# Linear attention and a highway layer on one core: stacked head pairs, permuted model dimensions, output summed and turned on TensorE, fixed instruction order

## The chip, the cores and the metric

The kernel runs on one core of a Trainium2 chip. Such a core has five engines with an instruction queue each: TensorE (PE, matrix products, its weight loads listed as PEld), VectorE (DVE), ScalarE (ACT), GpSimd (POOL) and SyncE (SP, which here only issues transfers). An engine works through its own queue in order and waits on semaphores for the others. Data lie in SBUF (128 partitions) and in PSUM (eight banks, written by PE); transfers between memory and SBUF run on 16 DMA engines. The metric is the device time of one execution in microseconds (us); less is better.

## The reference

Inputs are `q`, `k`, `v` of shape (8 batches, 8 heads, 576 tokens, 64) in fp32, two weight matrices of 512x512 and a bias of 512. First comes linear attention, then a highway layer on all 8 x 576 = 4608 tokens of 8 x 64 = 512 model dimensions:

```python
q_s = exp(q - max(q, -1));  q_s = q_s / sum(q_s, -1)      # softmax over the 64 dims
k_s = exp(k - max(k, 2));   k_s = k_s / sum(k_s, 2)       # softmax over the 576 tokens
kv  = einsum('bhsd,bhse->bhde', k_s, v)                   # 64 x 64 for each head
x   = einsum('bhsd,bhde->bhse', q_s, kv)                  # tokens x 512
H   = maximum(x @ w_h, 0)
T   = sigmoid(x @ w_t + b_t)
out = T * H + (1 - T) * x
```

The sums can be left to the end: dividing a row of `kv` by the sum of its `exp(k)` column is the same as normalising `k` first. A column of ones beside `v` gives that sum from the same product.

## The kernel before

A batch of 576 tokens is split into 512 (four tokens to a partition) and a rest of 64. `load_batch` (L77) fetches `k` and `q` as fp32 through SP's queue (q1 in the profile) and `v` through GpSimd's queue (q0), which casts it to fp16 on the way; the weights take the same queue (L215, L216). Three sets of input buffers exist. `prelude` (L97) does the exps on ScalarE and, on VectorE, the sums of the query softmax (`qsm`, L112, and `qst` for the rest), their reciprocals and the scaling (`qs16m`, L120).

Attention then goes pair by pair of heads, four pairs to a batch: PE forms `kv` of each head (L260, and L267 for the rest; 64x65 products, ten a pair), turns the scaled queries (L73) into the PSUM tile `qtt`, VectorE takes the reciprocal `rz` (L279), builds the block-diagonal `abk` of the two heads (L281 to L283) and copies the turned queries out as `qsT` (L285). `flush_rb` (L227) multiplies the two (`pxT`, L239), and ScalarE writes the result to `xT` (L247, L248), model dimensions on partitions, tokens along the free axis.

The highway layer works on blocks of 512 tokens, nine of them (`tcn`), which don't line up with the batches of 576. `moe_dc` (L141) takes one 128-wide part of the output dimensions: `psh` and `pst`, four products each (L148, L153); tanh in place of the sigmoid (`th`, L158, since sigmoid(z) = (1 + tanh(z/2))/2); `dd = max(psh, 0) - x` on VectorE (L161); `uu = dd * th` on GpSimd (L163). One part later `moe_flush_pend` (L167) does `ww = uu + dd` (L172) and `gg = 0.5 * ww + x` (L174) on VectorE. `moe_finish` (L177) turns `gg` back to token rows on PE (L73, `nat`), ScalarE copies the rows out (L191), and SP stores them, in 56 stores.

The order on the engines is that of a scheduler working from dependences and priorities; the code runs block `b-1` of the highway layer beside the attention of batch `b`, one part after each head pair, and `prelude(b+1)` after the first pair.

## Time and profile before

| | |
|---|---|
| time, median of 3 runs | 222.51 us (221.66 to 223.78) |
| span of the profiled execution | 219.1 us |
| median time less that span | 3.4 us |
| PE, DVE, ACT, POOL busy | 137.4, 164.5, 102.0, 79.5 us |
| read from memory, written | 30.41 MB, 9.44 MB |

The profile has the span of one execution, from its first to its last instruction; the time of a run holds a few microseconds around it. Busy times of the engines overlap, so they don't add up to the span; the longest of them is a floor, and what is above it are waits. In the rows of groups an entry reads line, engine, operation, output<-input, partitions x elements, count | busy us, mean ns of one | idle us ahead of them and what ended it. A row such as `PEclk` cuts the span into 40 slices of 5.5 us, one digit each.

### The profile page before, as it was taken

The numbers are of one execution on the slowest core, as the hardware profiler recorded it, in microseconds if no ns is written. First come the engines' busy times: TensorE is split into PE (matmuls) and PEld (weight loads), VectorE is DVE, ScalarE is ACT, GpSimd is POOL, SyncE is SP. The second block draws the span as 40 slices with busy tenths as digits, with TensorE's granted clock in tenths as the row PEclk, the third lists the DMA queues.
The fourth block names the chain that finished last, engine by engine and source line by source line (L and its number), as shares of the span: only waits on it lengthen the run. The fifth ranks groups of instructions, "written<-read, shape, count | busy, mean of one in ns | idle before, by whom it ended". The sixth has DMA issues, their size and how long they took to land.

```text
span 219.1 us, 3271 instructions
## 1 busy us (share of the span) xinstructions
PE 137.4 (63%) x1170; PEld 71.3 (33%) x1170; DVE 164.5 (75%) x357; ACT 102.0 (47%) x151; POOL 79.5 (36%) x84
## 2 busy tenths in 40 slices
...
PEclk9855558556999797699589959985996999999955
DMA  6999999999999999997899209920060033071426
GB/s 185 253 211 268 210 249 252 229 270 223 274 221 186 127 280 223 283 112 160 262 254 162 93 0 73 183 47 0 3 193 3 0 120 74 0 195 50 141 56 135
DMA packets 69696, 34.29 MB, mean 157 GB/s; under 512 B 47664, under 2 KB 65072, under 8 KB 69680
## 3 DMA queue, kind: packets, MB, share of 16 engines
q1 hardware_dynamic: 31120, 28.32, 50.4%
q0 software_dynamic: 38560, 5.77, 37.2%
q8 instruction: 9, 0.15, 0.3%
q14 instruction: 7, 0.06, 0.1%
HBM read 30.41 MB, written 9.44 MB: 182 GB/s over the span
## 4 chain that ended last, share of the span: by engine, by line
DVE 38%; DMA 30%; issue 13%; POOL 9%; PE 4%; ACT 2%; ACTq 1%; POOLq 0%; DVEq 0%
DMA v16m<-in_v_dram 30%; DVE gg L174 9%; POOL uu L163 5%; DVE dd L161 5%; DVE qsm L112 5%; DVE ww L172 5%; DVE qsT L285 4%; POOL v16m L88 3%; DVE qs16t L125 2%; DVE abk L283 2%; DVE qst L113 1%; DVE rz L279 1%; PE qtt L73 1%; DVE abk L282 1%; PE nat L73 1%
## 5 line engine op out<-in xcount | busy, mean ns | idle before, releaser
L163 POOL TENSOR_TENSOR uu<-dd,th 128x512 f16<-128x512 f16 x36 | 43.3, 1205 | 79.1 <-DVE dd L161 66.1
L153 PE MATMUL pst<-xT,w16t 128*128 128x512 f16 x144 | 44.8, 415 | 17.7 <-DVE dd L161 17.2
L148 PE MATMUL psh<-xT,w16h 128*128 128x512 f16 x144 | 42.2, 395 | 5.5 <-ACT th L158 3.5
...
L158 ACT ACTIVATE th<-pst,bt 128x512 f16<-128x512 f32 x36 | 24.9, 691 | 32.5 <-PE pst L153 32.5
L174 DVE SCALAR_TENSOR_TENSOR gg<-ww,xT 128x512 f16<-128x512 f16 x36 | 34.8, 966 | 0.3
L247 ACT CAST xT<-pxT 128x512 f16<-128x512 f32 x32 | 18.7, 583 | 27.7 <-PE qtt L243 27.5
L260 PE MATMUL qtt<-v16m,ek16m 128*64 128x65 f16 x256 | 17.6, 224 | 22.2 <-DMA v16m<-in_v_dram 21.4
L260 PEld LDWEIGHTS <-ek16m 128*64 128x64 f16 x256 | 12.4, 129 | 41.3 <-issue 41.1
L112 DVE TENSOR_REDUCE qsm<-eq16m 128x32 f16<-128x2048 f16 x8 | 18.2, 2277 | 9.8 <-ACT eq16m L105 9.7
L172 DVE TENSOR_TENSOR ww<-uu,dd 128x512 f16<-128x512 f16 x36 | 18.7, 520 | 9.0 <-POOL uu L163 8.7
L153 PEld LDWEIGHTS <-w16t 128*128 128x128 f16 x144 | 13.7, 102 | 35.0 <-issue 23.7
L105 ACT ACTIVATE eq16m<-q32m 128x2048 f16<-128x2048 f32 x8 | 15.3, 1907 | 21.0 <-DMA q32m<-in_q_dram 9.3
L161 DVE SCALAR_TENSOR_TENSOR dd<-psh,xT 128x512 f16<-128x512 f32 x36 | 23.9, 664 | 1.1 <-PE psh L148 1.0
L73 PE MATMUL nat<-ident,gg 128*128 128x128 f16 x144 | 16.3, 245 | 12.8 <-DVE gg L174 12.5
L191 ACT CAST o<-nat 128x1024 f32<-128x1024 f16 x18 | 17.4, 1016 | 12.9 <-PE nat L73 12.9
L73 PE MATMUL qtt<-ident,qs16m 128*64 128x128 f16 x256 | 22.5, 258 | 0.0
L103 ACT ACTIVATE ek16m<-k32m 128x2048 f16<-128x2048 f32 x8 | 15.4, 1920 | 13.2 <-DMA k32m<-in_k_dram 12.6
L279 DVE RECIPROCAL rz<-qtt 128x1 f32<-128x1 f32 x32 | 5.2, 162 | 20.0 <-PE qtt L73 19.8
L239 PE MATMUL pxT<-qsT,abk 128*128 128x512 f16 x32 | 14.9, 465 | 6.5 <-ACT xT L247 3.7
L148 PEld LDWEIGHTS <-w16h 128*128 128x128 f16 x144 | 13.2, 100 | 17.3 <-issue 6.3
L285 DVE TENSOR_SCALAR qsT<-qtt,rz 128x640 f16<-128x640 f16 x32 | 17.6, 550 | 1.0
...
## 6 DMA issues: line engine op xcount, KB each, us to landing
...
q32m<-in_q_dram SPq DMA_DIRECT2D x8, 1024.0 KB, 14.2
out_dram<-o SPq DMA_DIRECT2D x40, 128.0 KB, 2.4
v16m<-in_v_dram POOLq DMA_DIRECT2D x32, 128.0 KB, 10.2
out_dram<-o SPq DMA_DIRECT2D x16, 256.0 KB, 2.7
q32t<-in_q_dram SPq DMA_DIRECT2D x8, 128.0 KB, 11.4
k32t<-in_k_dram SPq DMA_DIRECT2D x8, 128.0 KB, 10.3
...
```

Of the source, the lines that this page charges most:

```text
L73: nc.tensor.matmul(out_ap, in_ap, idn, is_transpose=True, start=True, stop=True, skip_group_check=True,)
L88: nc.gpsimd.dma_start(v16m[:, :, j, 0:D], v_m[b][:, :, j, :])
L112: nc.vector.reduce_sum(qsm, eqm_g, axis=mybir.AxisListType.X)
L148: nc.tensor.matmul(psh, w16h[:, kc, dsl], xT[:, kc, tok], start=(kc == 0), stop=(kc == KC - 1),)
L153: nc.tensor.matmul(pst, w16t[:, kc, dsl], xT[:, kc, tok], start=(kc == 0), stop=(kc == KC - 1),)
L158: nc.scalar.activation(th, pst, AF.Tanh, bias=bt2[:, dc : dc + 1], scale=0.5)
L161: nc.vector.scalar_tensor_tensor(dd, psh, 0.0, xs, op0=ALU.max, op1=ALU.subtract)
L163: nc.gpsimd.tensor_mul(uu, dd, th)
L172: nc.vector.tensor_add(ww, uu, dd)
L174: nc.vector.scalar_tensor_tensor(gg, ww, 0.5, xs, op0=ALU.mult, op1=ALU.add)
L260: nc.tensor.matmul(psk[od, :], ek16m[:, h, j, :], v16m[:, h, j, 0 : D + 1], start=(j == 0), stop=False,)
L285: nc.vector.tensor_scalar_mul(qsT, pqt, rz)
```

## The change

The computation is the same; nearly every step is laid out anew.

*Loads.* Partition `64x + p` of an input tile holds head `2c + x`, tokens `9p` to `9p + 8`, for the four pairs `c`, so that nine tokens of a head (2304 bytes) are one piece and no rest of 64 tokens is treated apart. `v` comes as fp32 through SP's queue like `k` and `q`, and GpSimd casts it (`cast_v`, two halves a batch); the weights likewise (`cast_weight`, eight casts in all). GpSimd does nothing else in the main loop.

*Attention.* The exps work on halves of a batch (two head pairs on 128 partitions). `kv_half` forms products of 64 rows by 128 columns by 129: two heads at once, of which only the diagonal blocks are used. `q_sums` adds the halves of 64 in fp16 and reduces 32; `q_mult` scales in place; `q_trans` turns the queries in full 128x128 blocks. `x_blk` is the product with `abk`. The model dimensions stand in another order than in memory (within four heads, the odd ones behind the even ones), which the weights' loading and the order of the output's columns take back.

*Highway layer.* A block of 512 tokens now belongs to one batch (tokens `9p + n` for n up to 7), eight blocks, and the ninth tokens of all batches form the ninth block (`x9`). `moe_step` does tanh on ScalarE, then `dd` and `u = (th + 1) * dd`, both on VectorE. `out_tile` lets PE add and turn in one: `x` times the identity plus `u` times half the identity, summed in PSUM in fp32; ScalarE copies (two tiles of the last four go to VectorE), and SP stores four tokens to a partition at a time, 12 stores.

*Order.* `manual_schedule` keeps the order in which the code issues: in step s (0 to 3) of block c the four engines get `moe_step(c, s)`, quarter s of the attention of batch c+1, quarter s of the exps of batch c+2, and one output tile of an earlier pair of batches. Loads for batch c+3 are issued at the start of block c.

VectorE, around the sums of the query softmax of one batch, before: the two reductions and the scaling come in one piece, and the four small operations of a head pair stand between `dd`, `ww` and `gg`.

```order
L112 TENSOR_REDUCE qsm<-eq16m 128x32
L113 TENSOR_REDUCE qst<-eq16t 64x8
L116 RECIPROCAL rqm<-qsm 128x32
L117 RECIPROCAL rqt<-qst 64x8
L120 TENSOR_TENSOR qs16m<-eq16m,rqm 128x2048
L125 TENSOR_TENSOR qs16t<-eq16t,rqt 64x512
L126 MEMSET qs16t 64x256
L279 RECIPROCAL rz<-qtt 128x1
L281 MEMSET abk 128x64
L161 SCALAR_TENSOR_TENSOR dd<-psh,xT 128x512
```

VectorE after the change, the first half of block 1, with the number of a buffer behind each name: the sums of batch 2 (`l`, `r`) end just ahead, and the scaling of its queries (`eq_470`) stands two MoE steps later.

```order
L198 CAST r_2_508<-r_2_507 128x72
L268 SCALAR_TENSOR_TENSOR dd_0_531<-ph_0_520,xT_305 128x512
L271 SCALAR_TENSOR_TENSOR u_345<-th_0_529,dd_0_531 128x8x64
L268 SCALAR_TENSOR_TENSOR dd_1_568<-ph_1_557,xT_305 128x512
L271 SCALAR_TENSOR_TENSOR u_345<-th_1_566,dd_1_568 128x8x64
L178 RECIPROCAL rz_589<-psk_534 128x4
L182 TENSOR_TENSOR abk_108<-psk_534,rz_589 64x2x2x64 x2
L206 TENSOR_TENSOR eq_470<-eq_470,r_2_508 128x1280
L206 TENSOR_TENSOR eq_470<-eq_470,r_2_508 128x1024
L268 SCALAR_TENSOR_TENSOR dd_2_609<-ph_2_598,xT_305 128x512
```

So the reduction and the scaling of one batch are apart by two MoE steps, and each `dd` is followed at once by its `u`, where `ww` and `gg` waited for GpSimd.

GpSimd in the main loop before: products of the highway layer between the issues of the `v` transfers.

```order
L163 TENSOR_TENSOR uu<-dd,th 128x512 x2
L88 DMA v16m<-in_v_dram 128x8x64 x2
L163 TENSOR_TENSOR uu<-dd,th 128x512
L88 DMA v16m<-in_v_dram 128x8x64 x2
L91 DMA v16t<-in_v_dram 64x8x64
```

GpSimd after the change, from the first cast on.

```order
L156 CAST v_0_110<-v_0_117 128x9x128 x2
L112 CAST w16t<-w32t 128x8x64 x4
L112 CAST w16h<-w32h 128x8x64 x4
L156 CAST v_1_111<-v_1_135 128x9x128 x2
L156 CAST v_0_110<-v_2_341 128x9x128 x2
```

All that is left is casts, two a batch after the weights.

ScalarE at the end, before: two copies of two token tiles each, after four tanh in a row.

```order
L191 CAST o_2294<-nat_0_2060 128x1024
L191 CAST o_2300<-nat_1_2061 128x1024
L158 ACTIVATE th<-pst,bt_100 128x512 x4
L191 CAST o_2403<-nat_0_2305 128x1024
L191 CAST o_2407<-nat_1_2306 128x1024
```

ScalarE at the end, after the change (`o_3_4` is the buffer for tiles 4 to 7 of batches 6 and 7, `o_0_8` that for the ninth tokens of batches 0 and 1; the last number is the tile's own).

```order
L266 ACTIVATE th_2_1888<-pt_2_1878,bt_107 128x512
L296 COPY o_3_4_1902<-nat_4_1893 128x512
L296 COPY o_3_4_1902<-nat_5_1904 128x512
L266 ACTIVATE th_3_1924<-pt_3_1914,bt_107 128x512
L296 COPY o_3_4_1902<-nat_6_1929 128x512
L296 COPY o_3_4_1902<-nat_7_1939 128x512
L296 COPY o_0_8_1959<-nat_8_1950 128x512
L296 COPY o_2_8_1983<-nat_8_1974 128x512
```

Copies of one tile each, two to a step in the last block, and the tiles of the ninth tokens of all batches at the very end (those of pairs 1 and 3 on VectorE).

The added lines, with the constants, the weights' loading and the views of a block left out; the removed ones are the listing above.

```diff
...
+    def heads_view(t, b):
+        return t[b].rearrange("(c x) (p n) d -> (x p) c (n d)", x=2, n=N9)
...
+    ld = pool("ld", 3)
...
+    og = pool("og", 2)
+    ps_ht = pool("ps_ht", 3, space=PSUM)
+    ps_kv = pool("ps_kv", 1, space=PSUM)
+    ps_q = pool("ps_q", 2, space=PSUM)
+    ps_nat = pool("ps_nat", 1, space=PSUM)
+
+    ctx.enter_context(tc.manual_schedule())
...
+    def load(b, which, halves=1):
+        dst, src, tag = {
+            "k": (k32, k, "k32"), "q": (q32, q, "q32"), "v": (v32, v, "v32"),
+        }[which]
+        t = ld.tile([P, 4, N9, 64], FP32, tag=tag, name=f"{tag}_{b}")
+        dst[b] = t
+        view = heads_view(src, b)
+        step = 4 // halves
+        for c in range(0, 4, step):
+            nc.sync.dma_start(
+                t[:, c : c + step].rearrange("p c n d -> p c (n d)"),
+                view[:, c : c + step],
             )
...
+    def cast_weight(n):
+        o = w16[n].rearrange("p k (a x c d) -> p k a x c d", a=2, x=2, c=2)
+        i = w32[n].rearrange("p k (a c x d) -> p k a x c d", a=2, c=2, x=2)
+        for x in range(2):
+            for c in range(2):
+                nc.gpsimd.tensor_copy(o[:, :, :, x, c, :], i[:, :, :, x, c, :])
...
+    load(0, "k", 2)
+    load(0, "v", 2)
+    load(0, "q", 2)
+    load(1, "k")
+    load_weight("t", moe_w_t, "k32")
+    load_weight("h", moe_w_h, "q32")
...
+    load(1, "v")
+    load(1, "q")
...
+    def exp_half(b, which, a):
+        dst, src, p_, tag = {"k": (ek, k32, ekp, "ek"), "q": (eq, q32, eqp, "eq")}[which]
+        if a == 0:
+            dst[b] = p_.tile([P, N9, 4, 64], FP16, tag=tag, name=f"{tag}_{b}")
+        nc.scalar.activation(
+            dst[b][:, :, 2 * a : 2 * a + 2, :],
+            src[b][:, 2 * a : 2 * a + 2].rearrange("p c n d -> p n c d"),
+            AF.Exp,
+        )
+
+    def cast_v(b, a):
+        nc.gpsimd.tensor_copy(
+            v16s[b % 2][:, :, a, 0:128].rearrange("p n (c d) -> p n c d", c=2),
+            v32[b][:, 2 * a : 2 * a + 2].rearrange("p c n d -> p n c d"),
+        )
+
+    def kv_half(b, a):
+        if a == 0:
+            psk[b] = ps_kv.tile([P, 2, 512], FP32, tag="kv", name=f"psk_{b}")
+        t = psk[b]
+        for n in range(N9):
+            for x in range(2):
+                r = slice(64 * x, 64 * x + 64)
+                mm(
+                    t[:, x, 256 * a : 256 * a + 129],
+                    ek[b][r, n, 2 * a : 2 * a + 2, :].rearrange("p c d -> p (c d)"),
+                    v16s[b % 2][r, n, a, 0:129],
+                    n == 0, n == N9 - 1,
                 )
+
+    def kv_norm(b):
+        kvv = psk[b].rearrange("p x (a m) -> p x a m", a=2)
+        rz = small.tile([P, 2, 2], FP32, tag="rz", name=f"rz_{b}")
+        nc.vector.reciprocal(rz, kvv[:, :, :, 128])
+        ab = abks[b % 2].rearrange("p (a x) m -> p x a m", a=2)
+        for c in range(2):
+            r = slice(64 * c, 64 * c + 64)
+            nc.vector.tensor_mul(
+                ab[r, :, :, r], kvv[r, :, :, r], rz[r].broadcast_to([64, 2, 2, 64])
+            )
...
+    def q_sums(b):
+        e = eq[b].rearrange("p n c d -> p (n c) d")
+        l1 = small.tile([P, 4 * N9, 32], FP16, tag="l1", bufs=1, name=f"l1_{b}")
+        r32 = small.tile([P, 4 * N9], FP32, tag="r32", name=f"r32_{b}")
+        r2 = small.tile([P, 4 * N9, 2], FP16, tag="r2", name=f"r2_{b}")
+        qsum[b] = (l1, r32, r2)
+        with nc.allow_low_precision("fp16 pair sums of softmax terms"):
+            nc.vector.tensor_add(l1, e[:, :, 0:32], e[:, :, 32:64])
+            nc.vector.reduce_sum(r32, l1, axis=AX.X)
+        nc.vector.reciprocal(r32, r32)
+        nc.vector.tensor_copy(r2, r32.broadcast_to([P, 4 * N9, 2]))
+
+    def q_mult(b):
+        r2 = qsum[b][2]
+        e = eq[b].rearrange("p n c (w t) -> p (n c) w t", t=2)
+        rb = r2.unsqueeze(2).broadcast_to([P, 4 * N9, 32, 2])
+        half = 5 * 4
+        for s in (slice(0, half), slice(half, 4 * N9)):
+            nc.vector.tensor_mul(e[:, s], e[:, s], rb[:, s])
+
+    def q_trans(b, g):
+        if g == 0:
+            qsT[b] = qtp.tile([P, 4, N9, 64], FP16, tag="qsT", name=f"qsT_{b}")
+        ns = [(0, 4), (4, 8), (8, 9)][g]
+        w = ns[1] - ns[0]
+        t = ps_q.tile([P, 4, 4, 64], FP16, tag="qx", name=f"pq_{b}_{g}")
+        for n in range(*ns):
+            for a in range(2):
+                nc.tensor.matmul(
+                    t[:, 2 * a : 2 * a + 2, n - ns[0], :],
+                    eq[b][:, n, 2 * a : 2 * a + 2, :].rearrange("p c d -> p (c d)"),
+                    ident, is_transpose=True, start=True, stop=True,
+                    skip_group_check=True,
+                )
+        nc.vector.tensor_copy(qsT[b][:, :, ns[0] : ns[1], :], t[:, :, 0:w, :])
+
+    def x_blk(b, k_):
+        g, b2 = b // 2, b % 2
+        if k_ == 0 and b2 == 0:
+            xT[g] = xtp.tile([P, 4, NM, 2, 64], FP16, tag="xT", name=f"xT_{g}")
+        t = ps_q.tile([P, NM, 64], FP32, tag="qx", name=f"px_{b}_{k_}")
+        mm(
+            t.rearrange("p n d -> p (n d)"), abks[b % 2][:, k_, :],
+            qsT[b][:, k_, 0:NM, :].rearrange("p n d -> p (n d)"), True, True,
+        )
+        dst = xT[g][:, k_, :, b2, :]
+        if k_ < 3:
+            nc.scalar.copy(dst, t)
+        else:
+            nc.vector.tensor_copy(dst, t)
+
+    def x_left(b):
+        t = ps_q.tile([P, 4, 64], FP32, tag="qx", name=f"px_{b}_l")
+        for k_ in range(4):
+            mm(t[:, k_, :], abks[b % 2][:, k_, :], qsT[b][:, k_, NM, :], True, True)
+        nc.vector.tensor_copy(x9[:, :, b, :], t)
...
+    def moe_step(c, views, ob):
+        xv, uv = views
+        osl = slice(ob * P, ob * P + P)
+        pst = ps_ht.tile([P, 8, 64], FP32, tag="ht", name=f"pt_{c}_{ob}")
+        psh = ps_ht.tile([P, 8, 64], FP32, tag="ht", name=f"ph_{c}_{ob}")
+        for ps, w in ((pst, w16["t"]), (psh, w16["h"])):
+            for k_ in range(4):
+                mm(ps, w[:, k_, osl], xv(k_), k_ == 0, k_ == 3)
+        th = mo.tile([P, 8, 64], FP16, tag="th", name=f"th_{c}_{ob}")
+        nc.scalar.activation(th, pst, AF.Tanh, bias=bt2[:, ob : ob + 1], scale=0.5)
+        dd = mo.tile([P, 8, 64], FP16, tag="dd", name=f"dd_{c}_{ob}")
+        nc.vector.scalar_tensor_tensor(
+            dd, psh, 0.0, xv(ob), op0=ALU.max, op1=ALU.subtract
+        )
+        nc.vector.scalar_tensor_tensor(
+            uv(ob), th, 1.0, dd, op0=ALU.add, op1=ALU.mult
+        )
...
+    def out_tile(g, n, eng="act"):
+        if n < NM:
+            xs = lambda k_: xT[g][:, k_, n].rearrange("p b d -> p (b d)")
+            us = lambda k_: uu[g][:, k_, n].rearrange("p b d -> p (b d)")
+        else:
+            xs = lambda k_: x9[:, k_, 2 * g : 2 * g + 2].rearrange("p b d -> p (b d)")
+            us = lambda k_: u9[:, k_, 2 * g : 2 * g + 2].rearrange("p b d -> p (b d)")
+        t = ps_nat.tile([P, 2, 2, 2, 64], FP32, tag="nat", name=f"nat_{g}_{n}")
+        for k_ in range(4):
+            a, x = k_ // 2, k_ % 2
+            o = t[:, a, :, x, :]
+            mm(o, xs(k_), ident, True, False)
+            mm(o, us(k_), half_i, False, True)
+        q0 = n - n % 4
+        if n % 4 == 0:
+            o32[g, q0] = og.tile([P, 4, 512], FP32, tag="o32", name=f"o32_{g}_{n}")
+        o = o32[g, q0]
+        src = t.rearrange("p a c x d -> p (a c x d)")
+        if eng == "act":
+            nc.scalar.copy(o[:, n % 4, :], src)
+        else:
+            nc.vector.tensor_copy(o[:, n % 4, :], src)
+        rows = out.rearrange("(g p n) m -> g p n m", g=B // 2, n=N9)
+        if n % 4 == 3 or n == NM:
+            w = n - q0 + 1
+            nc.sync.dma_start(rows[g][:, q0 : q0 + w, :], o[:, 0:w, :])
...
+    def softmaxes(b):
+        return [
+            lambda: (exp_half(b, "k", 0), cast_v(b, 0)),
+            lambda: (exp_half(b, "k", 1), cast_v(b, 1)),
+            lambda: exp_half(b, "q", 0),
+            lambda: (exp_half(b, "q", 1), q_sums(b)),
+        ]
+
+    def attend(b):
+        return [
+            lambda: kv_half(b, 0),
+            lambda: (kv_half(b, 1), kv_norm(b), q_mult(b)),
+            lambda: (q_trans(b, 0), q_trans(b, 1), q_trans(b, 2)),
+            lambda: (x_blk(b, 0), x_blk(b, 1), x_blk(b, 2), x_blk(b, 3), x_left(b)),
+        ]
+
+    for f in softmaxes(0):
+        f()
+    cast_weight("t")
+    cast_weight("h")
     nc.vector.tensor_scalar_mul(bt2, bts, 0.5)
+    for f in attend(0):
+        f()
+    for f in softmaxes(1):
+        f()
+    loads(2)
+
+    for c in range(B + 1):
+        views = chunk(c)
+        att = attend(c + 1) if c + 1 < B else [None] * 4
+        sm = softmaxes(c + 2) if c + 2 < B else [None] * 4
+        if c + 3 < B:
+            loads(c + 3)
+        for s in range(4):
+            moe_step(c, views, s)
+            if att[s]:
+                att[s]()
+            if sm[s]:
+                sm[s]()
+            if c >= 2 and c < B:
+                out_tile(c // 2 - 1, 4 * (c % 2) + s)
+            elif c == B:
+                out_tile(3, 2 * s)
+                out_tile(3, 2 * s + 1)
+    for g in range(B // 2):
+        out_tile(g, NM, "act" if g % 2 == 0 else "dve")
...
```

326 lines of the change are left out of this document (72 added, 254 removed).

## The prediction

> **What bounds the kernel now.** The page's totals and slices first, then the DMA queues, the chain that ended last (its shares, and pieces of it in order of time: start, length, what), and two stretches of 20 us (after the range: us, busy us of PE, PEld, DVE, ACT, POOL, granted clock, DMA share, GB/s).
>
> ```profile
> span 219.1 us, 3271 instructions
> PE 137.4 (63%) x1170; PEld 71.3 (33%) x1170; DVE 164.5 (75%) x357; ACT 102.0 (47%) x151; POOL 79.5 (36%) x84
> PEclk9855558556999797699589959985996999999955
> DMA  6999999999999999997899209920060033071426
> GB/s 185 253 211 268 210 249 252 229 270 223 274 221 186 127 280 223 283 112 160 262 254 162 93 0 73 183 47 0 3 193 3 0 120 74 0 195 50 141 56 135
> q1 hardware_dynamic: 31120, 28.32, 50.4%
> q0 software_dynamic: 38560, 5.77, 37.2%
> HBM read 30.41 MB, written 9.44 MB: 182 GB/s over the span
> DVE 38%; DMA 30%; issue 13%; POOL 9%; PE 4%; ACT 2%; ACTq 1%; POOLq 0%; DVEq 0%
> ...
> 16.22 29.59 DMA v16m<-in_v_dram
> ...
> 46.46 22.84 DMA v16m<-in_v_dram
> ...
> 118.29 2.29 DVE qsm L112
> ...
> 138.92 2.29 DVE qsm L112
> ...
> 140.00:160.00 20.00, 15.31 (x136) 8.01 (x135) 19.45 (x44) 9.38 (x15) 4.71 (x4) 0.83 0.18 41
> 180.00:200.00 20.00, 17.01 (x123) 8.17 (x123) 17.32 (x32) 8.86 (x16) 8.47 (x7) 1.00 0.34 85
> ```
>
> There are two regimes. Up to about 69 us the chain is the v transfers. The 16 DMA engines are full, yet q0 (v and the weights, cast on the way, 38560 small packets) spends 37.2% of the span on 5.77 MB, while q1 moves 28.32 MB in 50.4%. From there to the end VectorE sets the pace: the reduction of the query sums comes back every 138.92 - 118.29 = 20.6 us, one batch, and VectorE is 19.45 us busy in a stretch of 20.
>
> **What the change does to the front.** q0 all but disappears: v comes as fp32 over q1 in pieces nine tokens long, and GpSimd casts it. The whole 30.41 + 9.44 = 39.85 MB then runs on q1. The rate is bounded below by q1's own, 28.32 MB in 50.4% of 219.1 = 110.4 us, 256 GB/s; I take the best slice, 283, since pieces are longer. The first batch step needs batches 0 and 1 (30.41 less 2.1 of weights is 28.3 MB, 3.54 a batch) and the weights ahead of `q32_1`: 9.18 MB, 32.4 us.
>
> ```profile
> L86 SPq DMA_DIRECT2D q32m<-in_q_dram x8: 548/3436/4542, 1.3 to 104.5; - x8
> out_dram<-o SPq DMA_DIRECT2D x40, 128.0 KB, 2.4
> out_dram<-o SPq DMA_DIRECT2D x16, 256.0 KB, 2.7
> ```
>
> Loads start at 1.3 us and a short transfer takes some 2 us, so `q32_1` is there at 35.8 us. Two exps (2.3) and the four sums instructions (2.7, priced below) stand ahead of the first `dd` on VectorE: 40.8 us. The weight casts, 8 on GpSimd behind data landed at about 28 us, are covered by this wait. Batch 0's own attention (sums 2.7, norm and scaling 2.4, copies 1.9 and about 3 of x) starts at 16 us and ends by 28, also covered.
>
> **Prices.** Rows by line (busy, mean ns), then by tile (min/median/max ns), then from the order of time.
>
> ```profile
> L112 DVE TENSOR_REDUCE qsm<-eq16m 128x32 f16<-128x2048 f16 x8 | 18.2, 2277 | 9.8 <-ACT eq16m L105 9.7
> L120 DVE TENSOR_TENSOR qs16m<-eq16m,rqm 128x2048 f16<-128x2048 f16 x8 | 18.3, 2291 | 0.0
> L116 DVE RECIPROCAL rqm<-qsm 128x32 f32<-128x32 f16 x8 | 2.7, 334 | 0.0
> L279 DVE RECIPROCAL rz<-qtt 128x1 f32<-128x1 f32 x32 | 5.2, 162 | 20.0 <-PE qtt L73 19.8
> L105 ACT ACTIVATE eq16m<-q32m 128x2048 f16<-128x2048 f32 x8 | 15.3, 1907 | 21.0 <-DMA q32m<-in_q_dram 9.3 <-DVE qsT L285 6.2 <-DVE qs16m L120 5.5
> L247 ACT CAST xT<-pxT 128x512 f16<-128x512 f32 x32 | 18.7, 583 | 27.7 <-PE qtt L243 27.5
> L158 ACT ACTIVATE th<-pst,bt 128x512 f16<-128x512 f32 x36 | 24.9, 691 | 32.5 <-PE pst L153 32.5
> masks.py:199 POOL TENSOR_SCALAR_AFFINE_SELECT ident<-ident 128x128 f16<-128x128 f16 x1 | 0.3, 304 | 0.1
> L174 DVE SCALAR_TENSOR_TENSOR gg<-ww,xT x36: 625/692/1853, 60.8 to 208.8; 128x512 f16<-128x512 f16 x36
> L161 DVE SCALAR_TENSOR_TENSOR dd<-psh,xT x36: 626/679/692, 50.4 to 205.9; 128x512 f16<-128x512 f32 x36
> L172 DVE TENSOR_TENSOR ww<-uu,dd x36: 410/415/1399, 60.0 to 208.4; 128x512 f16<-128x512 f16 x36
> L163 POOL TENSOR_TENSOR uu<-dd,th x36: 1148/1160/1615, 55.9 to 206.7; 128x512 f16<-128x512 f16 x36
> L285 DVE TENSOR_SCALAR qsT<-qtt,rz x32: 549/550/552, 24.7 to 184.8; 128x640 f16<-128x640 f16 x32
> 135.09 0.40 PE L73 MATMUL nat<-ident,gg 128*128 128x128 f16 x4
> 139.31 1.02 PE L153 MATMUL pst<-xT,w16t 128*128 128x512 f16 x4
> 206.69 1.20 POOL L163 TENSOR_TENSOR uu<-dd,th 128x512 f16<-128x512 f16 x1 [1.75 <-DVE dd L161]
> 206.91 1.52 DVE L174 SCALAR_TENSOR_TENSOR gg<-ww,xT 128x512 f16<-128x512 f16 x1
> ```
>
> *VectorE*, one batch step (one round of the main loop), with 0.15 us of each row taken as fixed (the 128x1 reciprocal takes 162 ns) and the rest scaled by elements. MoE: four `dd` at 0.67 and four `u` at 0.69, 5.4 us; `ww` and the step through GpSimd (`uu`) are gone, since `u` does both and TensorE adds the halves. Attention: `rz` 0.16, two norm products of 256 columns 0.42 each, `q_mult` 1280 + 1024 elements, three copies of the turned queries 0.79 + 0.79 + 0.31 (from `qsT`), x copies 0.67 + 0.40. Sums: pair add of 1152 at the pace of `ww` 0.76, reduction 1.35, reciprocal 0.36, spreading 0.2. No row shows `q_mult`'s operand, a pair repeated 32 times: at the pace of `ww` 1.52 us, at that of `qs16m` 2.70. I take 1.52, since like `ww` it reads neighbouring fp16 on both sides, where `rqm` was one fp32 spread out. Sum 5.4 + 5.5 + 2.7 = 13.6 us.
>
> *ScalarE*: four exps of 1152 (between 583 ns at 512 and 1907 at 2048: 1.14), four tanh, three x copies and four output copies at 0.58: 11.4 us. *TensorE* at full clock: four 512-column products take 1.02 with one tail, so 0.21 each, 1.7 us per MoE step; 128-column ones (0.40 - 0.22)/3 = 0.06: 36 for kv 2.2, 18 turns 1.1, x 1.0, 32 for the output 1.9: 13.0 us.
>
> VectorE leads with 13.6, but its order is fixed, so waits come on top. I lay one step along it:
> - after the copy of the third turned block it waits for PE's eight MoE products of step 3: 1.7;
> - the fourth x product needs a bank that ScalarE empties (two banks in `ps_q`): 0.7;
> - the sums wait for ScalarE's last exp, behind three x copies: 0.2;
> - after the first `u`, step 1's products come late, because they stand behind kv and an output tile on PE: 0.9.
>
> That is 3.5, so 17.1 us. Two terms follow.
>
> *GpSimd.* The last two rows show a `gg` that began at 206.91 while `uu` held on until 207.89, and took 0.9 longer than its median: a VectorE operation with two SBUF inputs stands until GpSimd is through. `dd`, with one input in PSUM, never exceeded 692 ns. The `uu` go, but two casts of v per step come. The nearest row with one input is the 128x128 select, 304 ns, less 0.1 fixed: 1.6 ns an element, 1.95 us for 1152 (by `uu` 2.5, as an upper end; a lower end is half the row, 1.0). The casts become ready with the end of kv 0 and kv 1, just ahead of `u` 0 and `q_mult`; the first falls into the wait of 0.9, the second costs 1.0 (0.2 to 2.5). [...]
>
> *Clock.* 0.83 in the steady stretch, 1.00 at 180 to 200 us. The row that differs is this one:
>
> ```profile
> PE pst L153 <- DVE dd L161: 17.2, 6, 4.0
> ```
>
> PE stood up to 4.0 us a batch behind VectorE's `qs16m`. In the new step its longest stand is about 1.6 us (behind `q_mult`). I take 0.92, 0.4 us a step on the parts of PE that VectorE waits for (0 to 0.7). [...]
>
> A step is 17.1 + 1.0 + 0.4 = 18.5 us.
>
> **The sum.** First `dd` of step 0 at 40.8. Seven steps, 129.5; less 0.9 (PE is ahead in step 0), less 1.3 (step 6 has no sums in front of the next `dd`), less 2.0 (no casts left): `dd` of step 7 at 166.1, PE 1.9 earlier, 164.2. Step 7 has only MoE and one output tile each, PE-bound: 4 x (1.7 + 0.5) = 8.8. Step 8 has two output tiles a step through the single `nat` bank (tile 0.5, copy and hand-over 0.85, tile 0.5): 4 x 3.55 = 14.2. So 187.2, and the last copy 0.85 later, 188.1. The output pool has two buffers: the DVE copy of tile (1,8) waits until the 1 MB store of (3,4) has landed. From 2.4 us at 128 KB and 2.7 at 256 that is 4.5, by 1.05 MB at 283 GB/s plus 2 it is 5.7; I take 5.1, 193.2. Then copy 0.7, store 2.4, copy 0.7 (tile (3,8), same wait), store 2.4, and 1.6 to the end: 201 us. The span before is 219.1 and the median time 222.5, so 3.4 lie around it: **204 us**, 8% below.
>
> **Rivals.**
> - *All the fast ends together*: transfers let the first `dd` come at 34 (ScalarE's exps are then the limit), `q_mult` and casts cost nothing beyond the waits, clock 1.0: 6.8, 5 x 1.0 and 7 x 0.4 less, 189. For it: longer pieces, no `uu`. Against: every hand-over between engines that I set at 0.1 can only be longer. 0.14.
> - *The transfers stay the limit*: the first 120 us of before average 222 GB/s, and if q1 keeps to that, batch 7 (30.41 MB and three stores ahead of it) lands at 154 us where step 5 wants it at 138: 220 us. Against: those slices carry q0's small packets. 0.06.
> - *Wide operations fall back to one element a cycle*: `q_mult` 2.70, the turned copies 1.2 + 1.2 + 0.4: 2.1 a step, 7 steps, 219 us. 0.06.
> - *Slower than before: PE at a low clock.* In the front of before the slices show 0.5 to 0.6. At 0.59 PE needs 13.0 / 0.59 = 22 us a step and becomes the bound; steps 7 and 8 stretch too, about 245 to 250 us. It turns to a loss once a step passes 20.5 us, below a clock of 13.0 / 20.5 = 0.63. For it: the output takes 288 products of 128 columns where 144 did, and the half-height kv products have no row of their own. Against: the clock was 0.83 and more wherever PE was three quarters busy. 0.04.
>
> **How the numbers follow.** My case has 0.70, 195 to 214 with its own bounds (transfers -7 to +3, casts -4 to +8 over five steps, clock -3 to +2). The range 189 to 218 leaves out half of the first rival and most of the last three. About 1%, 2.2 us, is what a measurement can tell from no change; 220.3 us and less is faster: 0.70 + 0.14 and half of the two near 220, 0.90; the same 0.04; slower 0.06.
>
> **What would show it.** Right: q0 near nothing and DMA busy from the start; first `dd` at 38 to 43 us; `l1` (L195) returning every 17 to 19 us; VectorE 75 to 85% busy in the steps; `u` (L271) and `q_mult` (L206) with maxima 1 to 2 us above their medians, `dd` without; L206 near 0.8 us; clock 0.9. Wrong: PE or DMA the releaser of most VectorE idle time, or a step longer than 20.5 us.

## The result and the profile after

The changed kernel takes **191.1 us** (median of 4 runs, 188.0 to 192.9) where the kernel before takes 222.1 beside it: a ratio of 0.855, interval 0.845 to 0.866. The forecast was 204, range 189 to 218. Medians are over all executions of a kernel, ratios and intervals over those that weren't in a slower state, which is why 191.1 over 222.1 isn't quite 0.855. The profiled execution was the fastest of the four, 188.0 us with a span of 185.9, and it is read against the forecast's span of 201.

The page of the changed kernel: span, engines, clock, transfer rate, the two main queues, the chain by engine.

```profile
span 185.9 us, 2831 instructions
PE 132.1 (71%) x1132; PEld 74.6 (40%) x1132; DVE 113.5 (61%) x190; ACT 92.9 (50%) x127; POOL 27.9 (15%) x36
PEclk9965555798599669999999999999999999999755
GB/s 207 305 394 263 224 267 392 391 392 391 392 391 391 392 238 4 0 0 2 290 406 293 192 338 398 123 173 0 0 229 2 0 141 88 197 28 226 205 138 115
q1 hardware_dynamic: 15600, 39.85, 60.4%
q0 software_dynamic: 128, 0.00, 0.1%
PE 36%; DVE 29%; DMA 18%; ACT 11%; SPq 3%; issue 2%; DVEq 0%; ACTq 0%
```

VectorE's work fell from 164.5 to 113.5 us and the chain that ended last now runs through PE first. q0 is all but empty; q1 moves all 39.85 MB in 60.4% of the span and reaches 391 GB/s in slices 7 to 14, far over the 283 of the best slice before.

Stretches of the same kernel, cut at the first `dd` of steps 0, 1, 4, 7 and 8 (us, busy us of PE, PEld, DVE, ACT, POOL, then granted clock, DMA share, GB/s):

```profile
38.30:55.90 17.60, 12.35 (x74) 5.39 (x74) 13.11 (x24) 8.11 (x11) 5.07 (x4) 0.81 1.06 392
55.90:73.70 17.80, 13.79 (x103) 6.57 (x101) 13.46 (x24) 9.02 (x12) 3.83 (x3) 0.81 0.71 264
105.80:121.60 15.80, 12.93 (x128) 7.22 (x126) 13.33 (x23) 10.78 (x16) 2.69 (x2) 1.00 0.82 292
152.10:160.80 8.70, 8.70 (x68) 4.91 (x66) 5.58 (x9) 5.09 (x8) 0.00 (x0) 1.00 0.30 122
160.80:185.90 25.10, 12.95 (x119) 8.80 (x116) 6.87 (x10) 7.91 (x13) 0.00 (x0) 0.77 0.40 162
```

The first `dd` starts at 38.3. Steps 0 and 1, which have no output tile yet, take 17.6 and 17.8 us at clock 0.81; a full step, with an output tile to each quarter, takes 15.8 at clock 1.0; and from `dd` of step 7 (152.1) to the end are 33.8.

In order of time, one full step on TensorE and VectorE (start, length, what; in brackets how long the engine stood before it and what released it), and under it TensorE's waits of that whole step (total us, times, longest):

```profile
110.75 1.11 PE L216 MATMUL pq<-ident,eq 128*128 128x128 f16 x16 [0.51 <-DVE eq L206]
113.47 0.27 PE L216 MATMUL pq<-ident,eq 128*128 128x128 f16 x2 [1.61 <-DVE qsT L222]
115.95 0.69 DVE L268 SCALAR_TENSOR_TENSOR dd<-ph,xT 128x512 f16<-128x512 f32 x1 [1.74 <-PE ph L61]
...
PE pq L216 <- DVE qsT L222: 1.6, 1, 1.6
PE pq L216 <- DVE eq L206: 0.5, 1, 0.5
PE px L61 <- ACT xT L235: 0.5, 1, 0.5
PE px_l L61 <- ACT xT L235: 0.2, 1, 0.2
```

TensorE is 12.93 us busy in a step of 15.80 and stands 0.51 + 1.61 + 0.46 + 0.18 = 2.8 us in it. That the two make up the step is bookkeeping: VectorE's 13.33 us of work, its wait of 1.74 and 0.7 us between its instructions do so too. The 1.61 is TensorE's longest stand. Two turns of the ninth token need a PSUM bank that VectorE has to empty first, and behind them in TensorE's queue are an output tile and the fourth product group, for which VectorE then waits 1.74.

What sets the step is a round that goes through both engines. The next step, in which no cast runs, shows it by three starts:

```profile
123.24 0.69 DVE L268 SCALAR_TENSOR_TENSOR dd<-ph,xT 128x512 f16<-128x512 f32 x1
129.33 0.27 PE L216 MATMUL pq<-ident,eq 128*128 128x128 f16 x2 [1.61 <-DVE qsT L222]
139.10 0.69 DVE L268 SCALAR_TENSOR_TENSOR dd<-ph,xT 128x512 f16<-128x512 f32 x1 [0.15 <-PE ph L61]
```

From the second `dd` of the step (123.24) VectorE works without a wait, through norm, scaling and the third `dd`, to the first copy of the turned queries, for which TensorE's two turns stand. From there (129.33) TensorE goes through an output tile, the fourth product group, the x products and the first two groups of the next step, for which the second `dd` of that step waits (139.10). That is 6.1 + 9.8 = 15.86 us. The rest of VectorE's step, with the wait of 1.74 and the sums, runs beside TensorE's part. This is the reading that the experiments bear out.

### The profile page after: what moved, and what is told of

Same layout as the page of the kernel before. It is cut to its first block, busy times and chain, and to the rows that moved or that the text cites. A ratio compares the mean times of both kernels' runs of the same rounds, so it can differ in the third digit from the quotient of the medians.

```text
span 185.9 us, 2831 instructions
## 1 busy us (share of the span) xinstructions
PE 132.1 (71%) x1132; PEld 74.6 (40%) x1132; DVE 113.5 (61%) x190; ACT 92.9 (50%) x127; POOL 27.9 (15%) x36
## 3 DMA queue, kind: packets, MB, share of 16 engines
q1 hardware_dynamic: 15600, 39.85, 60.4%
## 4 chain that ended last, share of the span: by engine, by line
PE 36%; DVE 29%; DMA 18%; ACT 11%; SPq 3%; issue 2%; DVEq 0%; ACTq 0%
PE ph L61 12%; PE pt L61 12%; PE nat L61 8%; DMA w32t<-in_moe_w_t_dram 8%; DMA q<-in_q_dram 7%; DVE u L271 7%; DVE dd L268 6%; ACT xT L235 6%; DVE eq L206 5%; DVE abk L182 3%; DMA out_dram<-o 3%; ACT eq L149 2%; DVE qsT L222 2%; ACT o L296 2%; DVE r L196 2%
## 5 line engine op out<-in xcount | busy, mean ns | idle before, releaser
L296 ACT COPY o<-nat 128x512 f32<-128x512 f32 x34 | 19.9, 584 | 37.0 <-PE nat L61 31.7
L61 PE MATMUL ph<-xT,w16h 128*128 128x512 f16 x128 | 35.5, 403 | 3.3 <-POOL w16h L112 1.7
L61 PE MATMUL pt<-xT,w16t 128*128 128x512 f16 x128 | 36.4, 411 | 0.4 <-ACT th L266 0.4
L266 ACT ACTIVATE th<-pt,bt 128x512 f16<-128x512 f32 x36 | 24.7, 686 | 19.3 <-PE pt L61 18.7
L268 DVE SCALAR_TENSOR_TENSOR dd<-ph,xT 128x512 f16<-128x512 f32 x32 | 22.0, 689 | 19.3 <-PE ph L61 18.8
L156 POOL CAST v<-v 128x1152 f16<-128x1152 f32 x16 | 20.0, 1269 | 77.2 <-PE px L61 37.1
L271 DVE SCALAR_TENSOR_TENSOR u<-th,dd 128x512 f16<-128x512 f16 x36 | 27.6, 765 | 3.7
L149 ACT ACTIVATE eq<-q 128x1152 f16<-128x1152 f32 x16 | 18.5, 1160 | 14.2 <-DMA q<-in_q_dram 14.2
L61 PE MATMUL nat<-half_i,u 128*128 128x128 f16 x144 | 21.1, 227 | 0.0
L149 ACT ACTIVATE ek<-k 128x1152 f16<-128x1152 f32 x16 | 18.4, 1156 | 3.1 <-DMA k<-in_k_dram 3.1
L61 PE MATMUL nat<-ident,xT 128*128 128x128 f16 x128 | 17.8, 220 | 2.7 <-ACT o L296 2.7
## 6 DMA issues: line engine op xcount, KB each, us to landing
w32t<-in_moe_w_t_dram SPq DMA_DIRECT2D x4, 256.0 KB, 14.4
```

The source lines that it names most:

```text
L61: mm = lambda o, l, r, st, sp: nc.tensor.matmul(o, l, r, start=st, stop=sp, skip_group_check=True)
L149: nc.scalar.activation(dst[b][:, :, 2 * a : 2 * a + 2, :], src[b][:, 2 * a : 2 * a + 2].rearrange("p c n d -> p n c d"), AF.Exp,)
L156: nc.gpsimd.tensor_copy(v16s[b % 2][:, :, a, 0:128].rearrange("p n (c d) -> p n c d", c=2), v32[b][:, 2 * a : 2 * a + 2].rearrange("p c n ...
L266: nc.scalar.activation(th, pst, AF.Tanh, bias=bt2[:, ob : ob + 1], scale=0.5)
L268: nc.vector.scalar_tensor_tensor(dd, psh, 0.0, xv(ob), op0=ALU.max, op1=ALU.subtract)
L271: nc.vector.scalar_tensor_tensor(uv(ob), th, 1.0, dd, op0=ALU.add, op1=ALU.mult)
```

## The experiments

Ratios are to the kernel before, measured beside each kernel; times are medians.

| kernel | us | ratio [interval] | span | full step at clock 1.0 |
|---|---|---|---|---|
| the change | 191.1 | 0.855 [0.845, 0.866] | 185.9 | 15.8 |
| casts off | 188.9 | 0.846 [0.838, 0.854] | 187.0 | 15.9 |
| fp32 scaling | 199.2 | 0.891 [0.886, 0.896] | 195.5 | 17.05 |
| v through GpSimd's queue | 207.4 | 0.935 [0.929, 0.942] | 204.4 | 15.86 |
| weights on two queues | 192.2 | 0.866 [0.863, 0.868] | 190.5 | 15.9 |
| products in steps 0, 1 | 189.6 | 0.856 [0.850, 0.861] | 188.1 | 15.85 |
| products in the gap | 185.6 | 0.833 [0.827, 0.839] | 183.4 | 15.86 |
| turns in the gap | 185.6 | 0.835 [0.831, 0.839] | not read | 15.86 |
| own tail buffers | 187.2 | 0.837 [0.829, 0.845] | 184.7 | 15.86 |
| sums early | 191.8 | 0.863 [0.859, 0.867] | 190.1 | 15.86 |
| third turns late | 180.7 | 0.810 [0.806, 0.814] | 179.5 | 14.65 to 14.83 |
| scheduler's order | 165.6 | 0.747 [0.744, 0.750] | 163.7 | 12.5 to 13.2 |
| scheduler, tail, queues | 159.2 | 0.716 [0.713, 0.720] | 155.7 | 12.5 to 12.8 |

### What sets the step

**Sums early, hand order kept.**

```diff
-            lambda: (exp_half(b, "k", 1), cast_v(b, 1)),
-            lambda: exp_half(b, "q", 0),
+            lambda: (exp_half(b, "k", 1), cast_v(b, 1), exp_half(b, "q", 0)),
             lambda: (exp_half(b, "q", 1), q_sums(b)),
+            lambda: None,
```

> The hand order is kept; in every step the exponentials of q and the sums of q's terms move one quarter earlier, so that the sums stand behind the third gate difference and ahead of the fourth, where VectorE waited 1.74 us for the fourth product group in the kernel after the change. Theory A (the scheduler's order was 22 us shorter in the span because work stands in that wait): VectorE has the sums (0.76 + 1.35 us and the two small ones) in the wait, steps of 15.85 become about 14.2, seven steps give 10 to 12 us, span about 175, time about 180. Theory B (the scheduler's gain comes from all its interleaving, the middle wait alone is taken by another): steps of 15.4 to 15.85, time 187 to 191.

The sums did go into the wait, and the step stayed at 15.86. VectorE now waits at the first and second `dd` of the next step instead, 1.17 + 1.34 us where it had waited 1.74 and up to 0.15. TensorE's four waits in the step from 124.6 to 140.5 read like the four rows above, to the tenth. The two waits of VectorE:

```profile
140.47 0.69 DVE L268 SCALAR_TENSOR_TENSOR dd<-ph,xT 128x512 f16<-128x512 f32 x1 [1.17 <-PE ph L61]
143.30 0.69 DVE L268 SCALAR_TENSOR_TENSOR dd<-ph,xT 128x512 f16<-128x512 f32 x1 [1.34 <-PE ph L61]
```

So filling VectorE's wait gains nothing: the sums belong to the part of VectorE's step that runs beside TensorE's, and TensorE's part and its stands stayed as they were. Theory A fell, and its successor was that the gain lies in TensorE's own stands.

**Third turn group late.** One edit, which moves the two turns on TensorE and, with them, VectorE's short copy of their result (0.28 us, now behind the fourth `u`):

```diff
-            lambda: (q_trans(b, 0), q_trans(b, 1), q_trans(b, 2)),
-            lambda: (x_blk(b, 0), ...
+            lambda: (q_trans(b, 0), q_trans(b, 1)),
+            lambda: (q_trans(b, 2), x_blk(b, 0), ...
```

> The hand order is kept, with one edit: the third group of turns of q (two products, whose result only the ninth token's x needs) stands on TensorE behind the fourth quarter's eight gate products instead of ahead of the third quarter's output tile. In the kernel after the change TensorE stood 1.61 us ahead of those two turns, for VectorE to copy the first group out of PSUM, and with it the output tile, the fourth product group and the fourth gate difference, which started 1.74 us late. Theory A (that place in TensorE's order is what lengthens the step): the products are done about 1.6 us earlier, steps of 15.85 become 14.1 to 14.4, seven steps give 10 to 12 us, span 174 to 177, time about 180. Theory B (as with the sums moved ahead, the wait comes back elsewhere, because VectorE and TensorE wait for each other in turn over the whole step and one place doesn't set it): steps of 15.4 to 15.85, time 186 to 192. The scheduler's order, which has many such moves at once, had steps of 12.5 to 13.6.

Steps of 14.65 to 14.83, 1.1 us less each; 180.7 us, 10 less than the change by the medians (the two profiled spans differ by 6.4). What A expected for the step (14.1 to 14.4) was 0.4 us too good, since some 0.7 us comes back: x products wait 0.3 to 0.4 us longer for ScalarE, and a new wait of 0.3 for the moved copy appears. TensorE's waits of the step from 117.5 to 132.1, and that step's busy times:

```profile
PE px L61 <- ACT xT L235: 0.7, 1, 0.7
PE pq L216 <- DVE eq L206: 0.5, 1, 0.5
PE px L61 <- DVE qsT L222: 0.3, 1, 0.3
PE px_l L61 <- ACT xT L235: 0.3, 1, 0.3
...
117.50:132.10 14.60, 12.77 (x127) 7.11 (x125) 12.81 (x23) 9.64 (x15) 0.00 (x0) 1.00 0.17 67
```

The stand of 1.61 is gone, and TensorE's stands are 1.8 us where they were 2.8. VectorE is 12.81 us busy in this step and no longer waits for the fourth product group, so that little is left to fill on either engine.

**Scheduler's order.** The line that records the order by hand is taken out, so that a scheduler orders the same operations.

```diff
-    ctx.enter_context(tc.manual_schedule())
```

> Undoes one part: the order by hand is off, and the scheduler orders the same operations, as in the kernel before. Theory A: the hand order keeps VectorE's idle time at 2.3 us a step; another order makes PE, ScalarE and VectorE meet worse, steps of 17 to 20 us, span 194 to 215. Rival B: the layout carries all of the gain, 183 to 190.

165.6 us, below what either theory had: the order written by hand costs 22 us of span and 25 of the median. By the starts of `dd`, 3 of the 22 are won by the end of step 0, 17 in steps 1 to 6 and 2 behind the first `dd` of step 8. The scheduler puts most of the fourth product group ahead of the last two turns, among other moves, and steps fall to 12.5 to 13.2 with TensorE nearly always busy. So it is in the last version of this section, which the same scheduler orders (two places of TensorE's order of time, and the stretch of a step), and where the trace shows no wait of TensorE between 102.9 and 115.4. Which of the scheduler's moves brings what wasn't run apart.

```profile
109.51 0.81 PE L60 MATMUL pt<-xT,w16t 128*128 128x512 f16 x3
110.46 0.27 PE L219 MATMUL pq<-ident,eq 128*128 128x128 f16 x2
...
102.90:115.40 12.50, 12.30 (x124) 7.02 (x120) 12.01 (x23) 9.50 (x15) 0.45 (x1) 1.00 0.19 77
```

**fp32 scaling.** The reciprocal is spread out as one fp32 value per 64 elements, as before the change, instead of as a repeated fp16 pair.

```diff
-            nc.vector.tensor_mul(e[:, s], e[:, s], rb[:, s])
+            ew = eq[b].rearrange("p n c d -> p (n c) d")
+            nc.vector.tensor_mul(
+                ew[:, s], ew[:, s], r32[:, s].broadcast_to([P, s.stop - s.start, 64])
+            )
```

> Undoes one part: the queries are scaled by the fp32 reciprocal spread over 64 elements, as in the kernel before, instead of by an fp16 pair repeated 32 times. Theory A: one element a cycle returns, 1.49 + 1.21 us for 0.83 + 0.68, and since PE waits for it in each step, each of 7 steps grows by 1.2: span 194 to 195. Rival B: the price returns but a wait of VectorE behind it (1.7 us ahead of the fourth dd) takes it in: under 3 us more.

The two instructions take 1.49 and 1.22 us instead of 0.83 and 0.68, in the first rows below the spread over all sixteen (min/median/max ns), of this kernel and of the change. TensorE's stands before the turns grow from 0.5 to 1.6 us (last row, the step from 111.8 to 128.9) and the step by 1.2, to 17.05. The repeated pair is worth 8 us, because the scaling lies in VectorE's part of the round, and not because VectorE is full.

```profile
L208 DVE TENSOR_TENSOR eq<-eq,r x16: 1218/1354/1493, 18.9 to 151.5; 128x1280 f16<-128x1280 f16 x8, 128x1024 f16<-128x1024 f16 x8
L206 DVE TENSOR_TENSOR eq<-eq,r x16: 683/755/826, 18.8 to 142.3; 128x1280 f16<-128x1280 f16 x8, 128x1024 f16<-128x1024 f16 x8
PE pq L220 <- DVE eq L208: 1.6, 2, 1.2
```

**Casts off.** The products of k and v then read the v of batches 0 and 1.

```diff
     def cast_v(b, a):
+        if b >= 2:
+            return
```

> Leaves out the casts of v from batch 2 on (12 of 16), so that the products of those batches use stale v; nothing else changes. Theory A (the prediction's price of 1 us a step, only smaller): a cast makes one VectorE operation with two SBUF inputs stand, and three such operations were long in the changed kernel (u at 1.23, 1.30 and 1.33 us for 0.69), of which those in steps 1 and 2 are followed by no wait: 0.5 to 1.5 us less in span, 184.4 to 185.4, and no u above 0.75. Rival B: casts also delay kv or the loads behind the scenes: 4 us or more less.

188.9 against 191.1 us, with intervals that overlap, and no shorter span: the casts cost no more than some 2 us in all, and possibly nothing. In the change itself a cast takes 1.15 us and a `u` that runs beside one up to 0.64 longer than its median; `dd`, with one input in PSUM, never. With the casts off, all 36 `u` took 0.69 (691 to 693 ns). The rows of the change:

```profile
L156 POOL CAST v<-v x16: 1142/1147/1605, 9.1 to 117.5; 128x1152 f16<-128x1152 f32 x16
L271 DVE SCALAR_TENSOR_TENSOR u<-th,dd x36: 692/693/1329, 39.1 to 172.0; 128x512 f16<-128x512 f16 x36
L268 DVE SCALAR_TENSOR_TENSOR dd<-ph,xT x32: 677/691/692, 38.3 to 158.6; 128x512 f16<-128x512 f32 x32
```

### The clock

Steps of some 17.5 us came at no fixed place: steps 3 and 4 with the casts off, none after step 1 in the profile of the change. Each has a stretch at half clock. Three kernels add work to TensorE: 28 products behind the second half of kv in steps 0 and 1, and 24 products or 24 turns in the 1.61 us gap of every step.

```diff
-            lambda: (kv_half(b, 1), kv_norm(b), q_mult(b)),
+            lambda: (kv_half(b, 1), kv_norm(b), q_mult(b), fill(b)),
...
+            for _ in range(28):
+                mm(t[:, 0:P], ident, ident, True, True)
```

> Adds 28 products of identity by identity on PE (into the free output bank) behind the second half of kv in steps 0 and 1, where PE idles 3.1 and 2.2 us; the output isn't touched. Theory A: these idle times are what drops the granted clock to one half in steps 0 and 1 (8 MoE products in 3.4 us where later steps take 1.7): the steps go from 17.5 and 17.8 to 15.9 to 16.2 us, the span 3 us lower, about 183. Rival B: the clock is low there for another reason (the start, the full DMA engines): steps unchanged or longer by what the 28 products add, span 186 to 188.

No gain (189.6), and steps 2, 4 and 5 took some 17.5 us too in its profile. The other two, whose `fill` differs in the call:

```diff
-            lambda: (q_trans(b, 0), q_trans(b, 1), q_trans(b, 2)),
+            lambda: (q_trans(b, 0), q_trans(b, 1), fill(b), q_trans(b, 2)),
...
+                mm(t[:, 0:P], ident, ident, True, True)
...
+                nc.tensor.matmul(t.bitcast(FP16)[:, 0:P], ident, ident, is_transpose=True, ...)
```

> Adds 24 plain products (identity by identity, into the free output bank, result unused) in each of the seven steps, between the second and the third group of turns, where PE idles 1.6 us behind VectorE's copy. Theory C: the granted clock falls to one half whenever a grid window of 3.41 us holds no plain product, and from the last MoE product of step 2 to the first of step 3 there are 3.2 to 3.6 us with turns alone, so that steps fall at random into 15.9 or 17.5 us. With products in the middle no window is empty: all seven steps at 15.5 to 16.0 us, no half clock between 50 and 170 us, span 181 to 184. Rival D: the low clock has another cause (VectorE's or the DMA engines' load, the phase of the run): steps of 17.5 still occur, span 186 to 190.

> As the run with 24 products in the gap, but the 24 are turns (the same instruction with its transpose flag), same place, same count. Theory C: turns don't count for the clock, so it behaves as the changed kernel does: some steps at 17.5 us and stretches of half clock after 55 us, span 185 to 190. Rival E: any instruction that keeps PE busy counts: no half clock after 50 us, as with the products.

Both took 185.6 us, with no half clock between step 1 and the tail in their profiles; work added where TensorE stands cost nothing and gained some 5 us. By the times and in the full steps, products and turns do the same, as rival E had it. (The profiled execution of the kernel with turns took 187.6 us, 2 more than the median, so nothing but its clock and TensorE's order is read.) Step 1 differs. First the kernel with products, then the one with turns, each in two stretches of 3.4 us, in which the clock is the third number from the end:

```profile
60.70:64.10 3.40, 3.13 (x31) 3.13 (x32) 2.83 (x5) 0.00 (x0) 1.22 (x1) 0.52 1.05 389
64.10:67.60 3.50, 2.93 (x17) 1.24 (x15) 1.68 (x3) 1.98 (x4) 0.00 (x0) 1.00 1.06 393
```

```profile
60.70:64.10 3.40, 2.58 (x26) 2.55 (x26) 3.26 (x5) 0.00 (x0) 0.25 (x1) 0.50 1.05 390
64.10:67.60 3.50, 3.50 (x17) 1.84 (x16) 0.40 (x2) 0.69 (x1) 0.00 (x0) 0.52 1.02 376
```

With products, TensorE busy for 3.13 us, the clock is back after one stretch; with turns, busy for 2.58 us, it is not. That doesn't tell whether a turn counts for less or whether 2.58 us of work was too little.

The time without a product doesn't decide it. In the change it is 64.04 - 59.02 = 5.0 us in step 1, followed by two stretches at half clock, and 113.58 - 110.25 = 3.3 in a full step, followed by none. But 81.87 - 77.61 = 4.3 us in step 2 was followed by none either, and with the casts off 96.04 - 92.71 = 3.3 us by one. What does sort the cases is all of TensorE's work, turns included, in stretches of 3.41 us laid on the grid on which the clock changes in each profile. Here are three such stretches, each with the next one below it: step 2 of the change, the 3.3 us with the casts off, and a full step of the kernel with turns, which holds a quarter of a microsecond of products at most:

```profile
78.88:82.30 3.42, 1.65 (x26) 1.50 (x27) 3.29 (x7) 0.00 (x0) 0.00 (x0) 1.00 0.00 0
82.30:85.71 3.41, 2.84 (x16) 1.19 (x14) 1.57 (x4) 2.53 (x5) 0.00 (x0) 1.00 0.01 2
...
92.73:96.14 3.41, 1.32 (x20) 1.17 (x21) 3.28 (x6) 0.89 (x1) 0.00 (x0) 1.00 1.03 397
96.14:99.55 3.41, 3.41 (x17) 1.72 (x14) 0.53 (x2) 1.27 (x2) 0.00 (x0) 0.50 0.98 362
...
94.75:98.17 3.42, 2.81 (x47) 2.65 (x48) 3.29 (x6) 0.75 (x1) 0.00 (x0) 1.00 1.05 400
98.17:101.58 3.41, 2.89 (x18) 1.27 (x16) 1.56 (x4) 2.35 (x5) 2.24 (x2) 1.00 0.94 349
```

The eleven kernels in hand order have 279 such stretches at full clock between 42 and 148 us. Half clock follows 26 of them: in 24 TensorE was busy for 1.03 to 1.57 us, in two, both with the third turns late, for 2.0. Full clock stays after the other 253, all with 1.61 us or more. By products alone the two groups overlap, against theory C. So a turn does count as work here (2.81 us of it, nearly all turns, and the clock stayed at 1.00 in the last pair above), and a full step, whose poorest stretch holds 1.3 to 1.8 us, falls on the one side or the other by where the grid lies. With products or turns in the gap no stretch after step 1 holds less than 2.0, and both keep the clock. With the 28 products the poorest stretches of those steps still held only 1.3 to 1.4 us. In step 1 half clock came after a stand of 2.15 us in the change and of 2.39 in the kernel with turns. The sorting was read off the traces afterwards and no run was made to test it; TensorE's busy times are in part modelled, so the limit of 1.6 us is rough, and the two cases at 2.0 stay open.

### The front and the end

**v through GpSimd's queue.** v is again cast by the transfer, in the new layout; loads of v leave SP's queue.

```diff
-        nc.gpsimd.tensor_copy(
-            v16s[b % 2][:, :, a, 0:128].rearrange("p n (c d) -> p n c d", c=2), ...
+            nc.gpsimd.dma_start(
+                v16s[b % 2][:, :, a, 64 * c : 64 * c + 64], view[:, 2 * a + c]
+            )
```

> Undoes one part: v goes through GpSimd's queue again and is cast on the way (four transfers a batch, pieces of 64 values), no casts on GpSimd; the rest is the changed kernel. Theory A: q0's pieces cost 81.5 us of the 16 engines for 38560 in the kernel before, 2.1 ns each, so 4608 a batch take 9.7 us beside 6 us for k and q at 392 GB/s: the transfers need about a step, 15.8 us, and delay the front and the middle: span 192 to 206. Rival B: loads run far enough ahead, v's path doesn't matter: 184 to 189.

The first `dd` moved from 38.3 to 59.5 and the full steps stayed as they were: v's path is worth some 16 us in the time and 21 in the front, and the middle doesn't feel it. Theory A was right on the front, more than it had reckoned, and wrong on the middle. Queue 0 of this kernel:

```profile
q0 software_dynamic: 37504, 4.72, 38.0%
```

**Weights on two queues.** In the change the rate dips to 222 GB/s while the weights load, each of whose loads fills 64 partitions, where long pieces run at 391. Here the halves for the upper 64 partitions go out through ScalarE's queue.

```diff
-        for c in range(2):
-            for a in range(2):
-                nc.sync.dma_start(flat[64 * c : 64 * c + 64, ...], src[a, c])
+        for a in range(2):
+            nc.sync.dma_start(flat[0:64, 2 * a : 2 * a + 2, :], src[a, 0])
...
+                nc.scalar.dma_start(flat[64:128, 2 * a : 2 * a + 2, :], src[a, 1])
```

> The hand order is kept; of each gate weight's four loads, which fill 64 partitions each, the two for the upper 64 partitions are issued by ScalarE behind the first two exponentials instead of by SyncE, so that loads of the lower and of the upper half are under way side by side. [...] Theory B (the dip comes from the pieces in DRAM or the packets' size): the front is the same within 1 us, time 190 to 192.

No gain: `dd` at 39.9, 192.2 us. Where the change moves 222 GB/s (first row below, a stretch of 4 us), this kernel moves 278 and then 132 (the rows under it): a quarter more in one stretch, and not the full rate of 391. The front is no shorter, as theory B had it, though what slows these loads stays open. The two halves met only in part: SyncE issued the second weight's lower half at 18.5 us, and v of batch 1 behind it at 25.3 instead of 18.9, with the dip to 132 just ahead of it.

```profile
22.00:26.00 4.00, 3.18 (x11) 1.01 (x11) 1.55 (x4) 2.81 (x5) 2.29 (x4) 0.50 1.09 222
...
18.00:22.00 4.00, 0.00 (x0) 0.00 (x0) 2.28 (x3) 1.16 (x1) 0.00 (x0) 0.50 1.07 278
22.00:26.00 4.00, 1.43 (x14) 1.47 (x15) 3.31 (x9) 0.00 (x0) 0.00 (x0) 0.50 0.70 132
```

**Own tail buffers.** The four ninth-token tiles of the output go to load buffers that are free by then, instead of to the two of the output pool.

```diff
-        if n % 4 == 0:
+        if n == NM:
+            t9 = ld.tile([P, 4, N9, 64], FP32, tag=("k32", "q32", "v32", "k32")[g], ...)
+            o32[g, q0] = t9.rearrange("p c n d -> p (c n d)")[:, 0:2048].rearrange(...)
+        elif n % 4 == 0:
```

> The four output tiles of the ninth tokens get buffers of their own (input buffers that are free by then) instead of the pool of two. Theory A: the two waits for stores at the end (5.0 us on VectorE, 5.2 us on ScalarE) go, and what is left is the bank, 1.25 us a tile: last copy at 178 instead of 182.4, span 181 to 182. Rival B: the last stores queue behind the 1 MB one anyway, so that the end moves by 2 us or less, 184 to 186.

In the change, a copy of VectorE stood 5.04 us for a store to land, as in the first two rows; here both last copies wait for TensorE alone. From the last `dd` to the last copy are 7.5 us (172.65 to 180.11) instead of 10.5 (171.16 to 181.70), 3 us saved of the 5, because the single `nat` bank is next. The span fell by 1.2 only, into B's range, because in this profile the last `dd` itself came 1.5 later; the mechanism is A's.

```profile
171.16 0.69 DVE L268 SCALAR_TENSOR_TENSOR dd<-ph,x 128x512 f16<-128x512 f32 x1 [2.01 <-PE ph L61]
177.68 0.69 DVE L298 COPY o<-nat 128x512 f32<-128x512 f32 x1 [5.04 <-DMA out_dram<-o]
...
176.94 0.69 DVE L303 COPY o<-nat 128x512 f32<-128x512 f32 x1 [2.80 <-PE nat L61]
180.11 0.69 DVE L303 COPY o<-nat 128x512 f32<-128x512 f32 x1 [2.48 <-PE nat L61]
```

**All of it on the scheduler's order**: tail buffers and two weight queues as above, and at the end every other output tile in a bank of `ps_kv`, which is free then.

```diff
-    ctx.enter_context(tc.manual_schedule())
...
+            t = ps_kv.tile([P, 2, 512], FP32, tag="kv", name=f"nat_{g}_{n}")[:, 0].rearrange(
```

> The scheduler's order (hand order off) with the weights' loads on two queues, output buffers of their own for the four ninth-token tiles, and in the last chunk and the tail a second PSUM bank for every other output tile. If the three savings add to the scheduler's 165.6 us: 4 us in the front, 3 us of store waits in the tail, and of 14.1 us of the last chunk some 2 to 4 us, so 155 to 158 us. If one of them is hidden: the loads, 40 MB at 391 GB/s being 102 us in all, have room; the last chunk is bound by ScalarE and VectorE together (copies and gates), then 159 to 161.

159.2 us, a ratio of 0.716: the fastest version here, within the second of the two cases. Of the 8 us less span than with the scheduler alone, 4 lie behind the first `dd` of step 8 (19.0 us instead of 23.0) and 2.6 in steps 0 to 2. The first `dd` came hardly earlier (31.3 and 31.7), so no run shows the 4 us set down for the front. What each of the three additions brings here wasn't run apart.

## Why the prediction was right, and where it was off

The direction held, and the range, by 2 us: the median lies outside the 195 to 214 that the main case had with a chance of 0.70, and the fastest execution, 188.0, below the range. The forecast's span was 15.1 us too long: 2.5 in the front, 11.5 in the seven steps, 1.1 at the end, all on the same side, so nothing cancelled.

*The front.* 40.8 was forecast for the first `dd`, 38.3 came. q0's disappearance was right, and the experiment with v shows that this is where the front was lost before. The rate was a mixture that 283 only happened to fit: 391 GB/s on the long pieces and 222 on the weights.

*VectorE's prices.* 13.6 us were forecast, 13.0 to 13.5 measured. The value taken for `q_mult` (1.52 of 1.52 to 2.70) came as 0.83 + 0.68, and its other end was measured as well: 1.49 + 1.22 = 2.71 in the fp32 kernel.

*"VectorE leads with 13.6, but its order is fixed, so waits come on top."* This is the step that failed. Laying a step along VectorE gave four waits, 3.5 us; one was right (1.74 for 1.7), another too (0.17 for 0.2), the x bank took 0.27 for 0.7, and step 1's products 0.15 for 0.9, 2.3 in all. The last was mis-sized in part because of the kv products, priced at 0.06 us each: eighteen of half height take 0.69 from the first start to the modelled end of the last, under 0.04 each (first row below). And the lead isn't VectorE's: the round goes along VectorE for 6.1 us of the step and along TensorE for 9.8, and TensorE had 13.0 us of products, forecast and found, and 2.8 us of stands. Of these the forecast named one, 1.6 us behind `q_mult`; that one was 0.5, and 1.6 stood behind a copy. The text called PE as releaser of most of VectorE's idle time a sign that it was wrong, and that sign came (second row, VectorE's longest wait over the span; between 38.3 and 160.8 PE released 21.3 of 22.1 us):

```profile
107.28 0.69 PE L61 MATMUL psk<-v,ek 64*128 64x129 f16 x18
...
DVE dd L268 <- PE ph L61: 25.5, 17, 3.1
```

Moving the sums into VectorE's wait shows it: nothing gained. Moving two turns on TensorE gained 6 us of span.

*GpSimd.* 1.0 us a step for the casts: too much. That a `u` is held up beside a cast was right (up to 0.64 us, and none with the casts off), the size not (1.15 us a cast, where 1.95 was taken), and what a cast adds to `u` falls in steps 3 and 4 on the fourth `u`, in the part of VectorE's step that runs beside TensorE's. In step 2 it fell on the second, 1.30 us for 0.69, and that step is 0.4 us longer than the others at full clock.

*The clock.* 0.4 us a step on average was forecast; steps 0, 1 and 2 were 1.7, 2.0 and 0.4 us over the 15.8 of the others, clock and casts together 4.1 where the two terms had 7.8 (7.0 + 2.8 less the 2.0 without casts). Full steps ran at 1.0, steps 0 and 1 at 0.81. The text had looked for gaps and found none over 1.6 us. By the reading above gaps aren't the measure: step 1 of the change, which has no output tile behind the turns, leaves a stretch of 3.41 us with 1.27 us of work.

*The end.* 34.9 us forecast, 33.8 measured; the 1 MB store, forecast as a wait of 5.1 us, cost 5.04 and 5.2.

*The rivals.* The time lies nearest to "all the fast ends together" (189): transfers and `q_mult` at their fast ends, casts near nothing, the clock at 1.0 in most steps. Transfers as the limit, slow wide operations and a low clock all through didn't happen: q1 ran at 391 GB/s, line 206 at 0.83 and 0.68, and the clock was 0.87 over the span. Two signs of being right stayed out: `l1` came back every 15.8 us instead of 17 to 19, and neither `u` nor line 206 had a maximum 1 us above its median (0.64 and under 0.1).
